# One TensorE body for all products: K and V by turns through one 32 KB buffer each, and wq, w1 and wo through the same two products

## The chip, the cores and the metric

The kernel runs on one core of one Trainium2 chip. The metric is the device time of one execution in microseconds (us). All numbers of a profile come from one profiled execution.

## The reference, cut to what matters

One decoding step for two rows of x. It mixes an attention over the last 4096 cached positions with a dense-Mish-dense block, by a sigmoid gate.

```python
# B, D, Hq, Hkv, Sk, Dh, F = 2, 512, 32, 8, 32768, 128, 1792;  W = 4096;  all fp32
q = (x @ wq).reshape(B, 1, Hq, Dh)                       # wq (512, 4096)
k, v = k_cache[:, :, Sk-W:], v_cache[:, :, Sk-W:]        # 8 heads, each used by 4 query heads
p = softmax(einsum("bhqd,bhkd->bhqk", q, k) * Dh**-0.5)
a = einsum("bhqk,bhkd->bhqd", p, v).reshape(B, 1, Hq*Dh) @ wo     # wo (4096, 512)
h = x @ w1 + b1                                          # w1 (512, 1792)
b = (h * tanh(softplus(h))) @ w2                         # w2 (1792, 512)
g = sigmoid((x * gate_w).sum(-1, keepdims=True))
out = g * a + (1 - g) * b
```

All of it is read once: 67 MB of K and V, 8.4 MB each of wq and wo, 3.7 MB each of w1 and w2, 91 MB together.

## The kernel before

**Layout.** Everything is stored for the kernel in rows, one to each of the 128 SBUF partitions. Three buffers `a`, `b`, `c` take 64 KB a partition each. K and V of one key-value head (both batch rows) stand side by side in one row of 64 KB (`kv_in[kv]`): the first 8192 numbers are K, the others V. Heads go by turns into `a` and `b`. `c` holds one half of wq, then the other, and at last w1, the first part of wo and a part of w2 (`w12`); the rest of wo follows in `a`, the rest of w2 in the end of `c`.

**The queue of loads.** All loads are issued by SyncE (SP), in the order of the code, by `load`. A load waits for a stage of TensorE (`"v0"`: the product with V of head 0 is done), so that its buffer is free; whatever stands behind it waits as well. The loads of heads 2 to 7 are issued while the load of another head is still on its way.

**TensorE.** `product` makes one output tile of 128x512 out of 16 matmuls: four column groups of 32 (`j`), each the sum over four chunks (`k`). In `step`, head `kv` goes through: wait for q (`q_in`) and for the data; the scores `sc`, 16 matmuls; `turn`, four transposes of the exponentials `p`; the product with V into `o`, 16 matmuls. `weights` does the same product with a half of wq or with w1, with x in the place of q. `ahead` runs over weights, two times two heads, weights, two times two heads, weights. `behind` is written out: the merge of the partial softmaxes (`lp`, `ol`), wo as 32 matmuls (`project`), w2 as 7 more and 7 blocks that are added up at the end (`finish`). An outer loop of two turns (`go`) passes over both parts once before it runs them.

**The other engines.** For each head VectorE takes the maxima of the scores (`mx`), ScalarE the exponentials and their sums, ScalarE copies the transposed `pT`, and after each second head VectorE picks the wanted parts of `o` (`om`, `od`, two heads in one instruction). After the last head `mx` is transposed (`mt`), the factors of the partial sums go over ScalarE, VectorE and GpSimd (`ms`, `top`) and back through TensorE (`ft`). Then `kf`, `kl` and the sums `lp` follow. Semaphores such as `q_in`, `p_in` and `pT_in` carry these hand-overs; the stages' names are counted in `STAGES`.

**The end.** The last three loads are pieces of w2 of 1 MB, 0.5 MB and 0.25 MB. After the last one `finish` ends, VectorE copies `fin` into `res`, and SP stores it.

Of the kernel before, what the change touches and what calls it, by code (L numbers as in the profile page):

```python
# [11 lines left out]
B = 2  # L12
# [17 lines left out]
FG = 4  # L30
HALF = 4
CHUNK = 8192
SMALL = DC * B + DC + FC
SCALE = DH ** -0.5
CAP = 20.0
CUTS = (0, 7, 11, 13, 14)
WO = (1, 6, 8)
ROWS = (24, 104)
WIDE = 2 * Q - B
STEP = Q + REP  # L40
TAIL = (FC - (NJ - 1) * FG) * P
GAPS = DC * (FG * P - TAIL) // D
FILLED = CHUNK + WO[0] * REP * D + (CUTS[1] - GAPS) * D

STAGES = ["gate"]
for _half in range(HKV // HALF):
    STAGES += [f"x{_half}s", f"x{_half}t"]
    for _kv in range(_half * HALF, (_half + 1) * HALF):
        STAGES += [f"s{_kv}", f"t{_kv}", f"v{_kv}"]
STAGES += ["tops", "factors", "x2s", "x2t", "shares", "outputs", "acc", "fin"]  # L50
# [3 lines left out]
class Line:  # L54
# [5 lines left out]
    def __call__(self, after, which, *args, credit=None, **kw):  # L60
        for mark in after[:-1]:
            self.e.wait_ge(*mark)
        ins = getattr(self.e, which)(*args, **kw)  # L63
        if after:
            ins._wait_ge(*after[-1])
        if credit is not None:
            ins.then_inc(credit, 1)
            return None
        ins.then_inc(self.sem, 1)
        self.n += 1  # L70
        return self.sem, self.n


def decode(nc, stored, small, wq, kv_in, w12, wo, w2, out):
    def sbuf(name, *shape):
        return nc.alloc_sbuf_tensor(name, [shape[0], *shape[1:]], F32).ap()
# [6 lines left out]
    a, b, c = (sbuf(n, P, 2 * CHUNK) for n in "abc")  # L83
# [8 lines left out]
    pick = sbuf("pick", P, BN)  # L92
    xg = sbuf("xg", P, DC, B)
    xs = sbuf("xs", P, B)
    g = sbuf("g", P, B)
    omg = sbuf("omg", P, B)
    qT = sbuf("qT", P, HKV, B, REP)
    p = sbuf("p", P, 512)
    pT = sbuf("pT", P, NT, P)
    om = sbuf("om", P, 2 * BN, DH)  # L100
# [7 lines left out]
    kl = sbuf("kl", P, HKV, BH)  # L108
    r = sbuf("r", P, HKV, B, REP)
    h, e, nu, de, ho = (sbuf(n, P, FC, B) for n in ("h", "e", "nu", "de", "ho"))  # L110
    sizes = (DC * Q, 2 * BN * STEP, HQ * Q, CUTS[1] * Q, (FC - CUTS[1]) * WIDE, WIDE)
    padded = sbuf("padded", P, sum(sizes))
    x32, qz, oT, actT, act2, fold2 = (
        padded[:, sum(sizes[:k]) : sum(sizes[: k + 1])] for k in range(len(sizes)))
    x32 = x32.rearrange("p (c q) -> p c q", q=Q)
    qz = qz.rearrange("p (y q) -> p y q", y=2)
    oT = oT.rearrange("p (k q) -> p k q", q=Q)
# [3 lines left out]
    sc = [bank(f"sc{y}", P, 512) for y in range(2)]  # L121
    pair = bank("o", P, 2, BN * DH)
# [3 lines left out]
    fb = bank("fb", P, 512)  # L126
    fin = fb[:, :P]
    zp = qb[:, :B]
    mt = qb[:HKV, 8 : 8 + P]
    ft = qb[:, 136 : 136 + HKV]  # L130
    lp = qb[:, 144 : 144 + HKV * BH].rearrange("p (k b h) -> p k b h", b=B, h=REP)
    ol = fb[:, P : P + HKV * BH].rearrange("p (k b h) -> p k b h", b=B, h=REP)

    names = ("data_a", "data_b", "data_c", "data_sm", "data_wo1", "data_wo2",
             "data_r1", "data_r2", "data_r3", "q_in", "p_in", "pT_in", "o_free")
    (d_a, d_b, d_c, d_sm, d_wo1, d_wo2, d_r1, d_r2, d_r3,
# [20 lines left out]
    load(b, kv_in[3], d_b, "v1")  # L157
    load(a, kv_in[4], d_a, "v2")
    load(b, kv_in[5], d_b, "v3")
    load(a, kv_in[6], d_a, "v4")  # L160
    load(b, kv_in[7], d_b, "v5")
    load(c[:, :FILLED], w12, d_c, "x1s")

    def flat(src, cuts, size):
        for f0, f1 in zip(cuts, cuts[1:]):
            yield (f1 - f0) * size, src[f0 * size * P : f1 * size * P].rearrange("(p x) -> p x", p=P)

    x = 0
    for sem, (cols, src) in zip((d_wo1, d_wo2), flat(wo, [f - WO[0] for f in WO], REP * D)):
        load(a[:, x : x + cols], src, sem, "v6")  # L170
        x += cols
    x = FILLED
    for sem, (cols, src) in zip((d_r1, d_r2, d_r3), flat(w2, [f - CUTS[1] for f in CUTS[1:]], D)):
        load(c[:, x : x + cols], src, sem)
        x += cols
# [7 lines left out]
    x_in = pool([blank, small_in], "tensor_copy", x32[:, :, ::RS], xT)  # L183
# [7 lines left out]
    fold2_in = dve([blank], "tensor_copy", fold2[:, Q - B : Q], fold[:, ::RS])  # L191
    prod = dve([small_in], "tensor_tensor", xg, xT, gw[:, :, None].to_broadcast([P, DC, B]), op=ALU.mult)
    gate_in = dve([prod], "tensor_reduce", xs, xg.rearrange("p c b -> p b c"), axis=AX.X, op=ALU.add)
    act([pe("gate")], "activation", g, zp, AF.Exp, scale=-1.0)
    t = dve([(act.sem, act.n)], "tensor_scalar_add", g, g, 1.0)
    t = dve([t], "reciprocal", g, g)
    gates_in = dve([t], "tensor_scalar", omg, g, -1.0, 1.0, op0=ALU.mult, op1=ALU.add)
    dve.e.sem_inc(o_free, 1)

    def head_in(kv, after):  # L200
        window = qz[:, kv % 2, :].rearrange("p (b n x) -> p b n x", n=NH, x=Q + REP)[:, :, :, :REP]
        pool(after, "tensor_copy", window, qT[:, kv, :, None, :].to_broadcast([P, B, NH, REP]),
             credit=q_in)

    def queries(i):
        act([pe(f"x{i}s")], "activation", p, sc[0], AF.Copy, scale=SCALE, credit=p_in)
        qt = pt.rearrange("p h (k b x) -> p h k b x", k=HALF, b=B)[:, :, :, :, 0]
        done = dve([pe(f"x{i}t")], "tensor_copy", qT[:, i * HALF : (i + 1) * HALF],
                   qt.rearrange("p h k b -> p k b h"))
        for kv in (i * HALF, i * HALF + 1):  # L210
            head_in(kv, [done])

    def head(kv):
        top_in = dve([pe(f"s{kv}")], "tensor_reduce", mx[:, kv : kv + 1], sc[kv % 2], axis=AX.X,
                     op=ALU.max, negate=True)
        act([top_in], "activation", p, sc[kv % 2], AF.Exp, bias=mx[:, kv : kv + 1],
            accum_out=ls[:, kv : kv + 1], credit=p_in)
        act([pe(f"t{kv}")], "copy", pT, pt, credit=pT_in)
        if (kv + 2) % HALF > 1:
            head_in(kv + 2, [pe(f"s{kv}")])  # L220

    def parts(kv):
        ov = om.rearrange("p (k m) d -> p k m d", m=BN)
        t = dve([pe(f"v{kv}")], "tensor_tensor", ov, pair.rearrange("p k (m d) -> p k m d", m=BN),
                pick[:, None, :, None].to_broadcast([P, 2, BN, DH]), op=ALU.mult)
        dve.e.wait_ge(*t)
        dve.e.sem_inc(o_free, 1)
        dve([], "tensor_reduce", od[:, kv - 1 : kv + 1], ov.rearrange("p k m d -> p k d m"),
            axis=AX.X, op=ALU.add)

    for kv in range(HKV):
        if kv % HALF == 0:
            queries(kv // HALF)
        head(kv)
        if kv % 2 and kv < HKV - 1:
            parts(kv)

# [8 lines left out]
    parts(HKV - 1)  # L246
# [3 lines left out]
    kl_in = dve([kf_in], "tensor_tensor", kl, kf, ls[:, :, None].to_broadcast(wide), op=ALU.mult)  # L250

    act([pe("x2s")], "copy", p[:, :TAIL], sc[0][:, :TAIL])
    act([], "copy", p[: Q * (NJ - 1), TAIL:], sc[0][: Q * (NJ - 1), TAIL:], credit=p_in)
    t = dve([pe("shares")], "reciprocal", r, lp)
    r_in = pool([t], "tensor_tensor", r, r, g[:, None, :, None].to_broadcast([P, HKV, B, REP]), op=ALU.mult)
    ht = pt.rearrange("p k (j b x) -> p k j b x", j=NJ, b=B)[:, :, :, :, 0]
    for j0, j1, nk in ((0, NJ - 1, FG), (NJ - 1, NJ, FC - (NJ - 1) * FG)):
        f0, f1 = j0 * FG, (j1 - 1) * FG + nk
        h_in = dve([pe("x2t")], "tensor_tensor", h[:, f0:f1, :].rearrange("p (j k) b -> p j k b", k=nk),
# [3 lines left out]
    o_in = dve([r_in, pe("outputs")], "tensor_tensor",  # L263
               oT.rearrange("p (k h) (b x) -> p k b h x", h=REP, x=RS)[:, :, :, :, 0], ol, r, op=ALU.mult)
    e_in = pool([h_in], "tensor_scalar_min", e, h, CAP)
    e_in = act([e_in], "activation", e, e, AF.Exp)
    ho_in = pool([gates_in], "tensor_tensor", ho, h, omg[:, None, :].to_broadcast([P, FC, B]), op=ALU.mult)
# [5 lines left out]
    pool([t], "tensor_tensor", actT[:, :, ::RS], nu[:, : CUTS[1]], ho[:, : CUTS[1]], op=ALU.mult)  # L273
    a_in = pool([], "tensor_tensor", act2[:, :, Q - B : Q], nu[:, CUTS[1] :], ho[:, CUTS[1] :], op=ALU.mult)
    asum_in = act([pe("acc")], "copy", p, acc)
    res_in = dve([pe("fin")], "tensor_copy", res, fin)
    store = nc.sync.dma_start(out, res[ROWS[0] : ROWS[1]]).then_inc(stored, 16)
# [14 lines left out]
    def product(out, lhs, block, mark=True):  # L292
        for k in range(NT):
            for j in range(NJ):
                mm(out[Q * j : Q * j + Q], lhs(k, j), block(k * NJ + j),
                   k == 0, k == NT - 1, mark=mark and k == NT - 1 and j == NJ - 1)
# [7 lines left out]
    def cut(t, k):  # L304
        return t[:, k * 512 : (k + 1) * 512]
# [138 lines left out]
```

## Time and profile before

| what | value |
|---|---|
| time, median of 3 runs | 220.59 us (219.42 to 221.84) |
| profiled execution, its own time | 220.39 us |
| its span, first to last instruction | 217.3 us |
| TensorE clock granted, mean | 0.819 |
| DMA: moved, mean rate | 91.31 MB, 420 GB/s |
| busy: TensorE matmul / VectorE / ScalarE / GpSimd | 53% / 10% / 7% / 3% |

The span leaves 3.1 us of the time outside (220.39 - 217.3). Of the views used below, the page's DMA queue row gives packets, MB, and the packets' time as a share of the 16 DMA engines' time; a row of the timeline gives start, length, engine, line of the kernel, operation, tiles and shapes, and in brackets the idle time of the engine ahead of it with what ended it. `PEq` is TensorE's own instruction queue.

### The profile page before, as it was taken

The page shows a single profiled execution, that of the slowest core. Times are in us where ns is not written, and L with a number is a line of the kernel's source. Part 1 is how long each engine was busy: PE and PEld are TensorE (multiplying, and loading weights), DVE is VectorE, ACT ScalarE, POOL GpSimd, SP SyncE. Part 2 cuts the span into 40 slices and gives each one's busy share as a digit, 9 for nine tenths or more (in the row PEclk, how much of TensorE's full clock was granted, in tenths as well). Part 3 has the DMA queues.
Part 4 walks back from the last instruction along what each step waited for, and adds up shares of the span by engine and source line. Part 5 has one row for each costly group of instructions (what it writes and reads, how often), then busy time and mean ns, then how long its engine had stood idle before and what let it go on. Part 6 is the DMA issues. An engine that isn't in the chain of part 4 may idle for free. (4 is left out here: it accounts for less than half of the span.)

```text
span 217.3 us, 1875 instructions
## 1 busy us (share of the span) xinstructions
PE 115.0 (53%) x816; PEld 36.6 (17%) x816; DVE 22.5 (10%) x37; ACT 15.6 (7%) x34; POOL 7.2 (3%) x28
## 2 busy tenths in 40 slices
PE   0029108552954009533779752287065918748895
PEld 0011002110220002101122220012021202215232
DVE  1010000100004000100106010010501001071100
ACT  2000100200020000200010020002002000211001
POOL 4000000000000000000000000000000000011200
PEclk9999755995579655996669998579958797999699
DMA  7998989896999898989899999999999999898993
GB/s 287 392 488 386 555 386 410 386 555 302 483 398 555 386 410 386 555 386 410 386 519 422 398 398 446 495 398 398 434 507 398 398 476 434 358 479 377 422 417 134
DMA packets 2546, 91.31 MB, mean 420 GB/s; under 512 B 416, under 2 KB 496, under 8 KB 752
## 3 DMA queue, kind: packets, MB, share of 16 engines
q1 hardware_dynamic: 2544, 91.28, 97.7%
q8 instruction: 2, 0.03, 0.1%
HBM read 91.24 MB, written 0.04 MB: 420 GB/s over the span
## 5 line engine op out<-in xcount | busy, mean ns | idle before, releaser
L286 PE MATMUL sc<-a,padded 128*32 128x512 f32 x128 | 21.6, 835 | 32.2 <-PEq L283 32.2
L286 PE MATMUL sc<-b,padded 128*32 128x512 f32 x128 | 23.6, 905 | 26.8 <-PEq L283 26.8
L286 PE MATMUL o<-b,pT 128*32 128x512 f32 x128 | 17.4, 692 | 3.1 <-PEq L283 3.1
L63 DVE TENSOR_REDUCE mx<-sc 128x1 f32<-128x512 f32 x8 | 5.5, 692 | 122.8 <-PE sc L286 122.8
L286 PE MATMUL o<-a,pT 128*32 128x512 f32 x128 | 15.9, 642 | 3.1 <-PEq L283 3.1
L301 PE MATMUL pt<-ident,p 128*128 128x128 f32 x44 | 6.9, 280 | 16.2 <-PEq L283 16.2
L63 ACT ACTIVATE p<-sc,mx 128x512 f32<-128x512 f32 x8 | 5.5, 687 | 137.6 <-DVE mx L63 137.6
L286 PE MATMUL sc<-c,padded 128*32 128x512 f32 x96 | 13.8, 727 | 0.9 <-PEq L283 0.9
L286 PEld LDWEIGHTS sc<-a,padded 128*32 128x32 f32 x128 | 5.6, 147 | 46.7 <-issue 46.7
L286 PEld LDWEIGHTS sc<-b,padded 128*32 128x32 f32 x128 | 5.9, 157 | 44.1 <-issue 44.1
L301 PEld LDWEIGHTS pt<-ident,p 128*128 128x128 f32 x44 | 4.6, 141 | 26.6 <-issue 26.6
L286 PE MATMUL qb<-xs,ones 128*128 128x2 f32 x2 | 0.6, 362 | 14.7 <-DVE xs L63 14.7
L63 DVE TENSOR_REDUCE od<-om 128x256 f32<-128x1024 f32 x4 | 7.9, 1977 | 0.6 <-DVE om L63 0.6
L286 PEld LDWEIGHTS o<-b,pT 128*32 128x32 f32 x128 | 4.9, 126 | 12.9 <-issue 12.9
L63 DVE TENSOR_TENSOR om<-o,pick 128x1024 f32<-128x1024 f32 x4 | 4.9, 1220 | 21.0 <-PE o L286 21.0
L286 PE MATMUL acc<-a,padded 128*32 128x512 f32 x56 | 6.8, 594 | 0.0
L286 PEld LDWEIGHTS o<-a,pT 128*32 128x32 f32 x128 | 4.7, 118 | 11.6 <-issue 11.6
L63 POOL COPY padded<-qT 128x16 f32<-128x16 f32 x8 | 1.5, 198 | 129.9 <-DVE qT L63 70.0
L63 ACT COPY pT<-pt 128x512 f32<-128x512 f32 x8 | 4.7, 586 | 6.5 <-PE pt L301 6.5
L286 PEld LDWEIGHTS sc<-c,padded 128*32 128x32 f32 x96 | 3.6, 128 | 8.9 <-issue 8.9
L286 PE MATMUL acc<-c,padded 128*32 128x512 f32 x22 | 4.3, 851 | 0.8 <-POOL padded L63 0.5
L286 PEld LDWEIGHTS qb<-xs,ones 128*128 128x128 f32 x2 | 0.5, 310 | 14.7 <-DVE xs L63 14.7
(60 smaller groups left out, 29.1 us busy)
## 6 DMA issues: line engine op xcount, KB each, us to landing
c<-in_wq SPq DMA_DIRECT2D x2, 4096.0 KB, 27.0
c<-in_w SPq DMA_DIRECT2D x1, 6400.0 KB, 40.8
a<-in_wo SPq DMA_DIRECT2D x1, 5120.0 KB, 32.0
a<-in_wo SPq DMA_DIRECT2D x1, 2048.0 KB, 36.5
c<-in_w SPq DMA_DIRECT2D x1, 1024.0 KB, 38.5
c<-in_w SPq DMA_DIRECT2D x1, 512.0 KB, 39.3
c<-in_w SPq DMA_DIRECT2D x1, 256.0 KB, 39.4
a<-in_kv SPq DMA_DIRECT2D x4, 29.6
```

The source lines that it names most:

```text
L63: ins = getattr(self.e, which)(*args, **kw)
L286: ins = T.matmul(out, lhsT, rhs, start=start, stop=stop)
L301: ins = T.transpose(pt[:, k, :], p[:, k * P : (k + 1) * P], ident)
```

## The change

K and V of a head become two loads of 4 MB, in rows of 32 KB: every K goes into `k0`, every V into `v0`. K of the next head is loaded once the scores of this head are done (`s`), V once the product with V is done (`v`). The two halves of wq go through the same two products (the second one in the place of V), so do w1 and the second half of wo, and at last the first half of wo. TensorE's program is one loop of 11 turns with branches for what differs, and a short end; the loop of two turns that passed over the code is gone. x, q and the attention's output are spread into windows of one shape (`lq`, `pT`) by GpSimd. The parts of `o` are picked after every head instead of every second one. The merge makes the weighted sum over `od` by two matmuls of 64x512 (`acc`, `fb`), from which VectorE picks (`oc`) and sums (`os`) before a transpose (`ot`). The gate's sum comes out of the matmul `lp`. A part of w2 comes early (`early`), before w1.

The core of the diff:

```diff
-    a, b, c = (sbuf(n, P, 2 * CHUNK) for n in "abc")
+    k0, v0 = (sbuf(n, P, CHUNK) for n in ("k0", "v0"))
+    rest = sbuf("rest", P, FC * D)
...
-    load(c[:, :CHUNK], wq[0], d_c)
+    load(k0[:, :HEAD], wqh, d_first)
+    load(k0[:, HEAD:], wqt, d_k)
     load(sm, small, d_sm)
-    load(a, kv_in[0], d_a)
-    load(b, kv_in[1], d_b)
-    load(c[:, :CHUNK], wq[1], d_c, "x0s")
-    load(a, kv_in[2], d_a, "v0")
...
+    load(v0, wq1, d_v)
+    for kv in range(HKV):
+        load(k0, kv_in[kv, 0], d_k, f"s{kv - 1}" if kv else "xs")
+        load(v0, kv_in[kv, 1], d_v, f"v{kv - 1}" if kv else "xv")
+    load(*flat(CUTS[0], CUTS[1]), d_early)
+    load(k0, w1, d_w1, f"s{HKV - 1}")
+    load(v0, wo1, d_v, f"v{HKV - 1}")
+    nc.sync.wait_ge(d_w1, 16)
+    nc.sync.sem_inc(d_k, 16)
...
+        t = dve([pe(f"v{kv}")], "tensor_tensor", om, o.rearrange("p (m d) -> p m d", m=BN),
+                pick[:, :, None].to_broadcast([P, BN, DH]), op=ALU.mult)
         dve.e.wait_ge(*t)
         dve.e.sem_inc(o_free, 1)
...
+        od_in = dve([], "tensor_reduce", od[:, kv, :], om.rearrange("p m d -> p d m"), axis=AX.X, op=ALU.add)
...
+    gaps_in = act([(d_w1, 16)], "copy", rest[:, : GAPS * D].rearrange("p (k x) -> p k x", k=DC),
+                  k0.rearrange("p (k x) -> p k x", k=DC)[:, :, (NJ - 1) * FG_P + TAIL :])
...
+    nc.sync.wait_ge(*gaps_in)
+    x = SPLIT * NJ * D
+    load(k0[:, :x], wo0[: P * x].rearrange("(p x) -> p x", p=P), d_k, "ws")
+    load(k0[:, x:], wo0[P * x :].rearrange("(p x) -> p x", p=P), d_split)
+    for k, sem in enumerate((d_r1, d_r2, d_r3), 1):
+        load(*flat(CUTS[k], CUTS[k + 1]), sem)
...
+    with T.Fori(0, 11, 1) as u:
         take(q_in, 1)
...
+        take(d_k, 16)
+        product(sc, lq, k0, SPLIT)
+        with T.If(u < 10):
+            turns()
             take(o_free, 1)
...
+            take(pT_in, 1)
+            take(d_v, 16)
+            product(o, pT, v0)
+            with T.If(u == 0):
+                turns()
+            with T.If(u == 8):
+                merge()
+            with T.If(u == 9):
+                T.wait_ge(*gaps_in)
+                project(0, CUTS[1], {0: a_in, GAPS: (d_early, 16)})
...
+    project(CUTS[1], ACC, {CUTS[1]: (d_r1, 16)})
...
-    with T.Fori(0, 2, 1) as go:
-        with T.If(go == 1):
-            ahead()
-        with T.If(go == 1):
-            behind()
```

SP's queue behind the last two heads, before: the loads of heads 6 and 7 into `a` and `b`, then `w12`, wo in two pieces, w2 in three, and the store.

```order
9 L147 DMA a<-in_kv 128x16384
10 L147 DMA b<-in_kv 128x16384
11 L147 DMA c<-in_w 128x12800
12 L147 DMA a<-in_wo 128x10240
13 L147 DMA a<-in_wo 128x4096
14 L147 DMA c<-in_w 128x2048
15 L147 DMA c<-in_w 128x1024
16 L147 DMA c<-in_w 128x512
17 L277 DMA out<-res 80x128
```

The same place now, from K and V of the last head (rows 18 and 19) on: seven blocks of w2, w1, the second half of wo, the first half of wo in two pieces, w2's last five blocks, the store.

```order
18 L150 DMA k<-in_kv 128x8192
19 L150 DMA v<-in_kv 128x8192
20 L150 DMA rest<-in_w 128x3584
21 L150 DMA k<-in_w 128x8192
22 L150 DMA v<-in_wo 128x8192
23 L150 DMA k<-in_wo 128x6144
24 L150 DMA k<-in_wo 128x2048
25 L150 DMA rest<-in_w 128x1024 x2
26 L150 DMA rest<-in_w 128x512
27 L303 DMA out<-res 80x128
```

Row 23 now waits for the product with w1 (`ws`), because it writes the buffer that w1 stands in; before, `w12` and wo went into buffers that the last heads and wq had left.

VectorE behind the last head, before: the maxima's merge stands ahead of the picking of heads 6 and 7, and `r` is made straight from the sums.

```order
20 L63 TENSOR_REDUCE mx<-sc 128x1 x2
21 L63 TENSOR_TENSOR mj<-ms 8x64
22 L63 TENSOR_REDUCE top<-mj 8x16
23 L63 TENSOR_TENSOR om<-o,pick 128x1024
24 L63 TENSOR_REDUCE od<-om 128x256
25 L63 TENSOR_TENSOR kf<-key,qb 128x64
26 L63 TENSOR_TENSOR kl<-kf,ls 128x64
27 L63 RECIPROCAL r<-qb 128x64
```

VectorE at the same place now: the last head's picking stands first, and `oc` and `os` have come in.

```order
30 L63 TENSOR_TENSOR om<-o,pick 128x512
31 L63 TENSOR_REDUCE od<-om 128x128
32 L63 TENSOR_TENSOR mj<-ms 8x64
33 L63 TENSOR_REDUCE top<-mj 8x16
34 L63 TENSOR_TENSOR kf<-key,qb 128x64
35 L63 TENSOR_TENSOR kl<-kf,ls 128x64
36 L63 RECIPROCAL r<-qb 128x64
37 L63 TENSOR_TENSOR oc<-acc,own 64x512
38 L63 TENSOR_TENSOR oc<-fb,own 64x512
39 L63 TENSOR_REDUCE os<-oc 64x128
```

On TensorE the transpose that reads `os` stands ahead of the product with w1, so that product now comes behind this whole row of VectorE; before, it came right behind the transpose `ft`.

More of the change, by code (lines that the diff above doesn't have):

```diff
@@ L35 @@
 CAP = 20.0
-CUTS = (0, 7, 11, 13, 14)
-WO = (1, 6, 8)
+HALF = 4
+FG = 4
+FG_P = FG * P
+TAIL = (FC - (NJ - 1) * FG) * P
+GAPS = DC * (FG_P - TAIL) // D
+CUTS = (GAPS, 9, 11, 13, 14)
+ACC = 11
+SPLIT = 3
 ROWS = (24, 104)
 WIDE = 2 * Q - B
[L40 to L50, printed above, removed]
+SHIFT = P + REP
+STAGES = ["xs", "xt", "xv", "xt2"]
+for _kv in range(HKV):
+    STAGES += [f"s{_kv}", f"t{_kv}", f"v{_kv}"]
+STAGES += ["tops", "factors", "shares", "outputs", "turned", "ws", "wt", "ov", "early", "h0", "acc", "fin"]
 AT = {name: k + 1 for k, name in enumerate(STAGES)}
@@ L58, in __init__, with __call__ @@
         self.n = 0
-    def __call__(self, after, which, *args, credit=None, **kw):
+    def __call__(self, after, which, *args, credit=None, by=1, **kw):
         for mark in after[:-1]:
@@ L198, in decode @@
-    dve.e.sem_inc(o_free, 1)
-    def head_in(kv, after):
[L201 to L206, printed above, removed]
-        qt = pt.rearrange("p h (k b x) -> p h k b x", k=HALF, b=B)[:, :, :, :, 0]
[L208 to L211, printed above, removed]
@@ L215, in head @@
+    first = queries(0, sc, "xs", "xt", [])
+    second = queries(1, o, "xv", "xt2", [first])
+    empty = pool([pe("xs")], "memset", lq, 0.0)
+    head_in(0, [empty, second])
+    for kv in range(HKV):
+        top_in = dve([pe(f"s{kv}")], "tensor_reduce", mx[:, kv : kv + 1], sc, axis=AX.X,
                      op=ALU.max, negate=True)
-        act([top_in], "activation", p, sc[kv % 2], AF.Exp, bias=mx[:, kv : kv + 1],
+        act([top_in], "activation", p, sc, AF.Exp, bias=mx[:, kv : kv + 1],
@@ L217, in head @@
             accum_out=ls[:, kv : kv + 1], credit=p_in)
[L218 to L225, printed above, removed]
+        if kv < HKV - 1:
+            head_in(kv + 1, [pe(f"s{kv}")])
+        else:
+            empty = pool([pe(f"s{kv}")], "memset", lq, 0.0)
+            x_windows(lq, q_in, 2, [empty])
@@ L290, in mm, with turn, product @@
             ins.then_inc(pe_sem, 1)
-    def product(out, lhs, block, mark=True):
+    def turn(out, src, eye, after=None, mark=True):
+        ins = T.transpose(out, src, eye)
+        if after is not None:
+            ins._wait_ge(*after)
+        if mark:
+            ins.then_inc(pe_sem, 1)
+    def product(out, lhs, t, split=None):
         for k in range(NT):
+            if k == split:
+                take(q_in, 1)
             for j in range(NJ):
-                mm(out[Q * j : Q * j + Q], lhs(k, j), block(k * NJ + j),
-                   k == 0, k == NT - 1, mark=mark and k == NT - 1 and j == NJ - 1)
@@ L298, in turn, with turns @@
-    def turn():
+                x = k * NJ + j
+                mm(out[Q * j : Q * j + Q], lhs[:, x * Q : x * Q + Q], t[:, x * 512 : (x + 1) * 512],
+                   k == 0, k == NT - 1, mark=k == NT - 1 and j == NJ - 1)
+    def turns():
         take(p_in, 1)
         for k in range(NT):
-            ins = T.transpose(pt[:, k, :], p[:, k * P : (k + 1) * P], ident)
-        ins.then_inc(pe_sem, 1)
-    def cut(t, k):
-        return t[:, k * 512 : (k + 1) * 512]
-    def weights():
-        take(d_c, 16)
-        product(sc[0], lambda k, j: x32[:, k, :], lambda k: cut(c, k))
-        turn()
@@ L312, in step, with merge @@
-    def step(y, t, sem):
+            turn(pt[:, k, :], p[:, k * P : (k + 1) * P], ident, mark=k == NT - 1)
+    def merge():
+        turn(mt, mx, ident)
+        turn(ft, ms.rearrange("k j r -> k (j r)"), ident[:HKV, :HKV], after=ms_in)
+        mm(lp, ones, kl, True, True, after=kl_in, mark=True)
+        kw = kf.rearrange("p k x -> p (k x)")
+        for y, dst in enumerate((acc, fb)):
+            mm(dst[: HKV * BH], kw, od[:, y * half : (y + 1) * half, :].rearrange("p k d -> p (k d)"),
+               True, True, mark=y == 1)
+        turn(ot.rearrange("p k b h -> p (k b h)"), os_, ident[: HKV * BH, : HKV * BH], after=os_in)
@@ L313, in step, with block, project @@
+    def block(f):
+        return rest[:, f * D : (f + 1) * D]
+    def project(f0, f1, after):
+        for f in range(f0, f1):
+            mm(acc[Q * (f % NJ) : Q * (f % NJ) + Q], actT[:, f, :], block(f), f < NJ, f >= ACC - NJ,
+               after=after.get(f), mark=f == f1 - 1)
+    T.wait_ge(d_first, 16)
+    T.wait_ge(*one)
+    with T.Fori(0, 11, 1) as u:
         take(q_in, 1)
-        take(sem, 16)
-        product(sc[y], lambda k, j: qz[:, y, k * Q : k * Q + Q], lambda k: cut(t, k))
@@ new lines, in finish, with output @@
+    def finish(lhsT, rhs, first=False, last=False, after=None):
+        for j in range(NJ):
+            y = j % 2 * (Q - B)
+            mm(fin[Q * j : Q * j + Q, :], lhsT[:, y : y + Q], rhs[:, j * P : (j + 1) * P],
+               first, last, after if j == 0 else None, last and j == NJ - 1)
+    def output(k, sem):
+        for f in range(CUTS[k], CUTS[k + 1]):
+            finish(act2[:, f - ACC, :], block(f), first=f == ACC, last=f == FC - 1,
+                   after=(sem, 16) if f == CUTS[k] else None)
@@ L390 @@
+    output(2, d_r2)
+    finish(fold2, p, after=asum_in)
+    output(3, d_r3)
 def kernel(**inputs):
```

238 lines of the change are left out of this document (97 added, 141 removed).

## Prediction

> **What bounds the kernel now.** First the page: the span, the busy shares, the DMA queues, and the chain that ended last.
>
> ```profile
> span 217.3 us, 1875 instructions
> PE 115.0 (53%) x816; PEld 36.6 (17%) x816; DVE 22.5 (10%) x37; ACT 15.6 (7%) x34; POOL 7.2 (3%) x28
> q1 hardware_dynamic: 2544, 91.28, 97.7%
> q8 instruction: 2, 0.03, 0.1%
> DMA 18%; PE 3%; SPq 0%; DVE 0%; issue 0%
> ```
>
> No engine is busy for more than 53%, and the DMA engines are for 97.7%: the kernel is a stream of 91 MB. Both versions read the same bytes. The 2.3% that are left are 5 us, most of them at the two ends, so more than that can't be won; what can be lost is anything that leaves the queue empty. The last long piece of the chain is a load, which agrees.
>
> Then the cost of a load. I ask the DMA view for two stretches in which only one sort of packet starts: from 53 to 59.5 us the second half of wq (rows of 32 KB), from 63 to 76 us a head (rows of 64 KB).
>
> ```profile
> q1 hardware_dynamic: 87, 2.85, 101.5%
> q1 hardware_dynamic: 91, 5.96, 106.0%
> ```
>
> A packet of 32 KB takes 1.015 x 16 x 6.5 / 87 = 1.213 us of one DMA engine, one of 64 KB 1.060 x 16 x 13 / 91 = 2.423 us. A load of 128 rows gives each of 16 engines eight rows, so 4 MB take 9.7 us.
>
> **Smaller rows.** 64 rows of 64 KB per DMA engine (eight heads) become 128 of 32 KB: 64 x (2 x 1.213 - 2.423) = 0.2 us. There are 29 DMAs in place of 18, and some rows of 8 to 24 KB in place of 40 and 50 KB. I take +0.4 us for both, between 0 and 0.8.
>
> **One buffer each: does the queue run empty while heads stream?** K of the next head is issued when this head's scores are done. By then V of this head is on its way, 9.7 us of it. So it comes in time if the product plus the dead time from an issue to flowing data is under 9.7 us. The timeline of TensorE has the product: eight that follow an idle time of 5 us or more, and two that follow shorter ones.
>
> ```profile
> 15.24 6.59 PE L286 MATMUL sc<-c,padded 128*32 128x512 f32 x32
> 33.63 5.93 PE L286 MATMUL sc<-a,padded 128*32 128x512 f32 x32 [10.35 <-PEq L283]
> 41.27 0.63 PE L301 MATMUL pt<-ident,p 128*128 128x128 f32 x4 [1.71 <-PEq L283]
> 42.66 3.64 PE L286 MATMUL o<-a,pT 128*32 128x512 f32 x32 [0.77 <-PEq L283]
> 52.93 6.52 PE L286 MATMUL sc<-b,padded 128*32 128x512 f32 x32 [6.63 <-PEq L283]
> 62.56 5.12 PE L286 MATMUL o<-b,pT 128*32 128x512 f32 x32 [0.77 <-PEq L283]
> 81.89 5.69 PE L286 MATMUL sc<-a,padded 128*32 128x512 f32 x32 [14.21 <-PEq L283]
> 101.22 6.27 PE L286 MATMUL sc<-b,padded 128*32 128x512 f32 x32 [6.88 <-PEq L283]
> 139.88 5.71 PE L286 MATMUL sc<-b,padded 128*32 128x512 f32 x32 [8.26 <-PEq L283]
> 159.19 6.29 PE L286 MATMUL sc<-a,padded 128*32 128x512 f32 x32 [6.85 <-PEq L283]
> 178.61 5.12 PE L286 MATMUL sc<-b,padded 128*32 128x512 f32 x32 [5.00 <-PEq L283]
> ```
>
> After a long idle time the product takes 5.12 to 6.59 us, 6.0 in the mean of the eight; soon after other work 3.64 to 5.12. For the dead time, SP's first load, its store, and the landing times of `c`:
>
> ```profile
> 0.72 0.39 SPq L147 DMA_DIRECT2D c<-in_wq  x1
> out<-res SPq DMA_DIRECT2D x1, 40.0 KB, 1.5
> DMA to landing us min/median/max: 13.4/39.3/40.8
> q8 instruction: 2, 0.03, 0.4%
> ```
>
> The store of 40 KB on an empty queue lands after 1.5 us. The first load, also on an empty queue, lands after 13.4 us, of which 9.7 are its packets. The last row is the first 30 us again: two instruction packets, 0.004 x 16 x 30 = 1.9 us of DMA time, so about 0.95 us on an engine; with that off, 2.75 us stay. The dead time is between 1.5 and 2.75 us; I take 1.8, nearer to the store. Then a half of a head needs 6.0 + 0.1 + 1.8 = 7.9 of 9.7 us, and in the worst case 6.6 + 0.1 + 2.75 = 9.45. The queue stays filled, K and V alike (the exponentials and `pT` come 3 us after the scores, before V lands). The cover left is 1.8 us, 0.25 at worst; what it costs without it is the second rival. The two halves of wq at the start go through the same test.
>
> The Trainium skill speaks against smaller loads: "DMA: Bandwidth & Descriptors", section "Anatomy of one DMA", puts about 2.0 us of fixed cost on each DMA, mostly the confirmation of the last write. By that figure the cover would be 1.6 in place of 1.8 us; as a cost of every queued load it would be 11 x 2.0 = 22 us more, and the packet rows above, which leave no room between loads, speak against that reading.
>
> **The one place where the queue does run empty.** The first half of wo can be issued only after `ws`. From the moment T at which V of the last head lands, the queue still holds seven blocks of w2 (1.75 MB), w1 and the second half of wo (4 MB each): 4.2 + 9.7 + 9.7 = 23.6 us. Against it stands a chain. The rows for it are those of the old merge and two groups:
>
> ```profile
> 190.72 0.26 ACT L63 COPY ms<-qb 8x128 f32<-8x128 f32 x1 [4.03 <-PE qb L333]
> 191.01 0.21 DVE L63 TENSOR_TENSOR mj<-ms 8x64 f32<-8x64 f32 x1 [6.52 <-ACT ms L63]
> 191.26 0.24 DVE L63 TENSOR_REDUCE top<-mj 8x16 f32<-8x64 f32 x1
> 191.59 0.59 POOL L63 TENSOR_TENSOR ms<-ms,top 8x64 f32<-8x64 f32 x2 [45.71 <-DVE top L63]
> 192.21 0.31 ACT L63 ACTIVATE ms<-ms 8x128 f32<-8x128 f32 x1 [1.23 <-POOL ms L63]
> 192.57 0.22 PE L334 MATMUL qb<-ident,ms 8*128 8x8 f32 x1 [1.88 <-ACT ms L63]
> 194.95 0.22 DVE L63 TENSOR_TENSOR kl<-kf,ls 128x64 f32<-128x64 f32 x1
> 198.92 0.43 PE L286 MATMUL qb<-kl,ones 128*128 128x64 f32 x2
> 201.45 1.31 PE L286 MATMUL acc<-c,padded 128*32 128x512 f32 x8 [0.36 <-DVE padded L63]
> L63 DVE TENSOR_TENSOR om<-o,pick 128x1024 f32<-128x1024 f32 x4 | 4.9, 1220 | 21.0 <-PE o L286 21.0
> L63 DVE TENSOR_REDUCE od<-om 128x256 f32<-128x1024 f32 x4 | 7.9, 1977 | 0.6 <-DVE om L63 0.6
> ```
>
> - V's product, 0.1 + 6.0 us. Ahead of it TensorE idles some 3.7 us with the transposes in between, which no row shows exactly; the ends are 3.64 and 6.6.
> - `om` and `od` of one head, half the size: 0.6 + 1.0, with gaps 1.7 us. They now stand ahead of `mj`.
> - From `mj` to the end of `ft`: 191.01 to 192.79, 1.8 us; then `kf` and `kl` 0.5, `lp` 0.5: 2.8 us.
> - The two new matmuls of 64x512. No row has one. A product is eight groups of four matmul passes side by side, so (32 records for 16 matmuls) a pass of 512 columns takes 3.64 / 8 = 0.46 to 6.6 / 8 = 0.83 us, and two fp32 matmuls are four passes without a neighbour: 1.8 to 3.3 us. TensorE comes from 4 us with little work, so I take 3.3, with 0.2 for the hand-over 3.5.
> - `oc` twice 512 columns, as `om`: 1.25; `os` sums 1024, as `od`: 2.0; the transpose, the loop's jump and the next waits 0.7. Together 3.95 us.
> - The product with w1, after an idle time: 6.0 us.
>
> T to `ws`: 6.1 + 1.7 + 2.8 + 3.5 + 3.95 + 6.0 = 24.05 us. With 1.8 us of dead time, data flow 25.85 us after T, against 23.6 of cover: an empty queue for **2.2 us**. With all short ends (3.7, 2.0 for the matmuls, 5.1, dead time 1.5) it is 20.75 and no gap; with all long ones (6.7, 3.5, 6.6, 2.75) 28.0 and 4.4 us.
>
> Two of these terms hang on TensorE's clock after a pause. The rows: 3.64 us right after work, 5.12 to 6.59 after 5 us without. The Trainium skill, "TensorE: Matmul & The Clock Gate", section "Why this matters for your kernels", warns of idle gaps over about 3 us between bursts, after which the clock drops to half. By this rule V's product is slow, as I took it, and the gap stays 2.2; if 3.7 us with transposes in them don't count as idle, that product takes 3.64 and the gap is nothing.
>
> **What lies beside other work.** More, shorter `om` and `od` (eight pairs of 1.7 us for four of 3.2), GpSimd's windows, and the copy of w2's part by ScalarE stand beside TensorE's waits for data; without that cover the copy alone would be worth 1.2 us (1024 columns, ScalarE's 512 take 0.59). TensorE's end is the same: four short matmuls after the last 0.25 MB, `res`, the store.
>
> **Instruction packets.** A load is complete with its last engine, so a packet of 0.95 us that holds one engine delays all. TensorE's program shrinks from 175 matmuls to 73. If neither packet is left, 0.95 us is won; if one is, nothing. I take -0.3.
>
> **Sum**, on the profiled execution: 220.39 + 0.4 + 2.2 - 0.3 = **222.7 us**, with the 3.1 us outside the span unchanged. The profiled time stands 0.2 us below the median of the three runs, 220.59.
>
> **The rivals.** *No gap:* the chain to `ws` is short enough. 220.39 + 0.4 - 0.95..0 = 219.8 to 220.8. For it: 3.64 us is common in the trace; against it: nearly all of its short ends are needed together. *The queue runs empty in every half:* the second rival, on the slower side. It decides once product and dead time are over 9.7 us, that is a dead time over 3.0 us with the slowest products; the first load's full 3.7 us would do it. Then 18 halves lose 0 to 0.7 us each; at 0.4, with the gap 2 us longer, 222.7 + 7.2 + 1.9 = 231.8. Against it: the rows above give 2.75 at most. The skill's fixed cost, paid by every load, would fall under this rival. *The loop's jumps miss:* the change doesn't do what it says, and code is loaded again in the loop. At 0.95 us a time this hides in the cover of 1.8 us, except ahead of `ws`: 223.7 or more. Against it: before loops too, and shows two packets in all, both in the first 30 us. *Faster:* 97.7% leaves only the ends; both packets gone, no gap, a run at the low edge: 218.
>
> **How the numbers follow.** The forecast, a gap of 1 to 3.5 us: 0.55, with 221.3 to 224.3. No gap 0.26; empty in every half 0.09; missing jumps 0.04; faster 0.06. A measurement of this kernel tells about 1% from no change, 2.2 us: under 218.4 or over 222.8. The forecast's range lies about half over that: 0.27 same, 0.28 slower. With no gap (0.26, same) and the two slower rivals this makes 0.06 faster, 0.53 same, 0.41 slower. The range, 219.5 to 225.5, takes in the case without a gap and the long ends of the chain; the empty queue in every half is left out, and so are the faster case and the worst of the jumps.
>
> **What would show it.** One stretch with idle DMA engines, some 200 to 205 us into the span, ended by the issue of wo's first half right after `ws`; from 15 to 175 us a DMA share as before. `os` ends 11 to 12 us after the last V product. If the DMA share drops in each half, the second rival is right; if the chain from T to `ws` is under 22 us, the first. The forecast is wrong in kind if the queue's packet time changes, or if TensorE waits for its own program.

## The result, and the profile after

The changed kernel takes **228.87 us** (median of 4 runs, 228.23 to 229.89) against 220.2 us (median of 4, 219.42 to 221.84): a ratio of 1.0388, with a 95% interval of 1.0311 to 1.0465. It is slower, and outside the range of the prediction. The profiled execution took 228.28 us with a span of 226.4, at a granted clock of 0.827 (before 0.819). The ratios in this document leave out an execution in a slower state, more than 1.5% above the fastest of its kernel (e1_go and e6_own have one each, their highest time), which the medians and ranges still count.

The page of the kernel after: span, busy shares, the DMA and GB/s rows of the 40 slices (5.66 us each), and the queues.

```profile
span 226.4 us, 1928 instructions
PE 124.9 (55%) x779; PEld 37.0 (16%) x779; DVE 28.7 (13%) x54; ACT 16.6 (7%) x35; POOL 9.4 (4%) x34
DMA  6999999799999999999999999999999999997893
GB/s 250 434 429 452 399 431 457 289 446 365 440 330 440 376 457 417 411 457 376 434 417 446 399 440 434 423 434 394 417 440 440 405 420 454 452 446 259 360 404 155
q1 hardware_dynamic: 4128, 91.28, 96.0%
q8 instruction: 1, 0.02, 0.0%
```

The same 91.28 MB, now spread over a span that is 9.1 us longer. The DMA row shows a slice with a 7 from 40 to 45 us and a 7 and an 8 from 204 to 215; the GB/s row shows more than the tenths do: below 380 in slices 8, 10, 12, 14 and 19, all while heads stream. Stretches of 20 us make that readable, first of the kernel before, then of the one after (columns: window, length, busy time of PE, PEld, DVE, ACT and POOL, clock, DMA share, and last GB/s).

```profile
40.00:60.00 20.00, 10.79 (x68) 3.13 (x68) 0.80 (x2) 1.36 (x3) 0.20 (x1) 0.74 0.98 423
60.00:80.00 20.00, 5.75 (x36) 1.74 (x36) 3.37 (x3) 1.36 (x3) 0.00 (x0) 0.73 1.01 439
80.00:100.00 20.00, 9.96 (x68) 2.94 (x68) 0.69 (x1) 1.36 (x3) 0.00 (x0) 0.84 1.04 449
100.00:120.00 20.00, 15.50 (x102) 4.63 (x103) 3.95 (x3) 1.96 (x4) 0.00 (x0) 0.75 0.97 419
120.00:140.00 20.00, 8.49 (x76) 3.04 (x79) 0.88 (x2) 1.36 (x3) 0.53 (x3) 0.85 0.98 426
140.00:160.00 20.00, 10.67 (x72) 3.02 (x75) 3.85 (x3) 1.36 (x3) 0.20 (x1) 0.84 1.02 442
160.00:180.00 20.00, 12.52 (x76) 3.58 (x72) 0.69 (x1) 1.36 (x3) 0.00 (x0) 0.76 0.97 421
```

```profile
40.00:60.00 20.00, 11.56 (x72) 3.40 (x68) 2.43 (x3) 1.36 (x3) 0.24 (x1) 0.76 0.94 387
60.00:80.00 20.00, 11.38 (x72) 3.32 (x68) 2.43 (x3) 1.36 (x3) 0.24 (x1) 0.76 0.98 395
80.00:100.00 20.00, 10.18 (x76) 3.12 (x72) 2.42 (x3) 1.36 (x3) 0.24 (x1) 0.84 0.98 419
100.00:120.00 20.00, 10.49 (x76) 3.08 (x71) 2.43 (x3) 1.36 (x3) 0.24 (x1) 0.84 1.00 424
120.00:140.00 20.00, 12.58 (x80) 3.45 (x76) 2.43 (x3) 1.36 (x3) 0.24 (x1) 0.78 1.00 423
140.00:160.00 20.00, 11.75 (x80) 3.65 (x72) 2.42 (x3) 1.36 (x3) 0.24 (x1) 0.83 1.01 424
160.00:180.00 20.00, 11.12 (x68) 3.39 (x64) 2.42 (x3) 1.36 (x3) 0.24 (x1) 0.74 0.98 423
206.00:210.00 4.00, 3.15 (x24) 0.93 (x20) 0.25 (x2) 0.64 (x2) 0.45 (x2) 0.84 0.66 197
```

Between 40 and 180 us the mean was 431 GB/s before and is 414 now. Over 140 us that is 2.5 MB too little, or 5.7 us at the old rate. In single rows of before the rate swings too, since 64-KB packets are counted where they fall; its mean over the stretch is what compares. The DMA share hides most of this (it is 0.98 at 395 GB/s, and 1.01 at 439 before), since packets on engines that have just been refilled last longer: from 63 to 66 us 27 of 32 KB start at a share of 97.9%, so that one takes 0.979 x 16 x 3 / 27 = 1.7 us, where the prediction found 1.2 in a full stream. The last row is the one gap that was forecast: 206 to 210 us.

Where the 9.1 us of span are, from the same two traces: V of the last head is used from 185.34 us on, where the last head's scores began at 178.61 before; the same bytes have landed at both points, so 6.7 us are lost until then. 2.2 us are lost ahead of the first half of wo, and 0.2 at the end. Outside the span 1.9 us are left, where the profiled execution of before had 3.1. 6.7 + 2.2 + 0.2 - 1.2 = 7.9 us, and 220.39 + 7.9 is the measured 228.28. But the 1.2 us are no gain of the change: in 28 of 30 later executions of the kernel before 1.8 to 2.2 us lie outside the span, and 3.0 and 3.4 in the other two.

How a hole of the stream arises, in SP's rows (start, duration, the issue) beside TensorE's:

```profile
28.48 0.33 SPq L150 DMA_DIRECT2D v<-in_kv  x1
41.82 0.33 SPq L150 DMA_DIRECT2D k<-in_kv  x1
36.31 5.45 PE L312 MATMUL sc<-k,padded 128*32 128x512 f32 x32 [6.39 <-PEq L309]
```

K of head 0 is complete at 36.2 us on its last engine, the scores start at 36.31 and take 5.45 us, and K of head 1 is issued right after, at 41.82. By then V of head 0, issued at 28.48 and queued behind K, is about to end on 15 of 16 engines (landings from 41.9 to 42.4 us). This is the worst of the holes: K of head 1 lands 1.8 us late. Of the 16 loads of the heads eight are issued less than 2.8 us ahead of the drain, and lose 0.2 to 1.8 us each; of the other eight one loses 0.8 (at a lead of 2.9) and seven nothing (0.05 or less). The leads and losses here and below are read from the packets and landings of the 16 engines in the traces.

### The profile page after: what moved, and what is told of

Same layout as the page of the kernel before. It is cut to its first block, busy times and chain, and to the rows that moved or that the text cites. A ratio compares the mean times of both kernels' runs of the same rounds, so it can differ in the third digit from the quotient of the medians.

```text
span 226.4 us, 1928 instructions
## 1 busy us (share of the span) xinstructions
PE 124.9 (55%) x779; PEld 37.0 (16%) x779; DVE 28.7 (13%) x54; ACT 16.6 (7%) x35; POOL 9.4 (4%) x34
## 3 DMA queue, kind: packets, MB, share of 16 engines
q1 hardware_dynamic: 4128, 91.28, 96.0%
## 5 line engine op out<-in xcount | busy, mean ns | idle before, releaser
L312 PE MATMUL sc<-k,padded 128*32 128x512 f32 x352 | 62.4, 874 | 60.2 <-PEq L309 60.2
L312 PE MATMUL o<-v,padded 128*32 128x512 f32 x320 | 46.0, 727 | 15.9 <-PEq L309 15.9
L312 PEld LDWEIGHTS sc<-k,padded 128*32 128x32 f32 x352 | 16.1, 153 | 103.8 <-issue 103.8
L312 PEld LDWEIGHTS o<-v,padded 128*32 128x32 f32 x320 | 13.3, 129 | 41.9 <-issue 41.9
L63 DVE TENSOR_TENSOR om<-o,pick 128x512 f32<-128x512 f32 x8 | 5.5, 692 | 64.9 <-PE o L312 64.9
L63 DVE TENSOR_REDUCE od<-om 128x128 f32<-128x512 f32 x8 | 8.3, 1043 | 1.2
L63 POOL COPY padded<-qT 128x64 f32<-128x64 f32 x8 | 1.9, 236 | 137.9 <-PE sc L312 128.6
L63 ACT COPY padded<-pt 128x512 f32<-128x512 f32 x8 | 4.7, 585 | 6.5 <-PE pt L319 6.5
L63 POOL MEMSET padded<- 128x528 f32 (+2 forms) x4 | 3.1, 766 | 34.0 <-PE sc L312 26.9
L312 PE MATMUL acc<-rest,padded 128*32 128x512 f32 x22 | 3.8, 595 | 0.0
L63 DVE TENSOR_TENSOR om<-om,sc 128x512 f32<-128x512 f32 x1 | 0.7, 687 | 10.3 <-PE sc L312 10.3
## 6 DMA issues: line engine op xcount, KB each, us to landing
k<-in_wo SPq DMA_DIRECT2D x1, 3072.0 KB, 10.3
```

What stands on the lines that cost most here:

```text
L312: ins = T.matmul(out, lhsT, rhs, start=start, stop=stop)
```

## The experiments

Three theories stood against each other. **A:** a straggler; the one instruction packet of 16 KB at 33 us holds one DMA engine, and all later holes follow from that (a straggler is the engine that ends a load last). **B:** a load has to be issued about 3 us before the queue drains, not 1.8, and most halves don't have that. **C:** 32-KB packets in alternating buffers are slower by themselves. "Lead" is how long before the middle one of the 16 engines ends the packets of the load ahead the next load is issued; "loss" is by how much its landing there then comes later than 9.69 us after the landing ahead.

### e1_go: the code loaded before the stream

```diff
+    with T.Fori(0, 2, 1) as go:
+        with T.If(go == 1):
             <the first two waits and the loop of 11 turns>
+        with T.If(go == 1):
             <the short end>
```

> The new kernel with the old kernel's outer loop of two turns around TensorE's program, which passes over the code once before it runs it, so that the packet of code that held one DMA engine at 33 us comes while the first half of wq is loaded. Theory A (the straggler: that packet made one engine finish the first K 3.4 us after the others, and the queue's cover was lost from there on): the long idle stretch at 42 us goes and most of the later ones, 222.5 to 225. Theory B (a load needs some 3 us from its issue to flowing data while others are on their way, more than the 1.8 us that were taken, so halves with a slow product lose time with or without a straggler): the stretch at 42 us shrinks, others stay, 226 to 228. Theory C (packets of 32 KB that alternate between K and V are slower by themselves): no change, 228 to 229.

Measured: 230.26 us (227.72 to 233.12), ratio 1.0506 (1.0422 to 1.0589). The packet moved to 4.5 us, and the stretch from 40 to 60 us is whole again. The holes come back elsewhere:

```profile
40.00:60.00 20.00, 13.27 (x68) 3.54 (x68) 2.06 (x3) 1.24 (x3) 0.23 (x1) 0.66 1.01 433
60.00:80.00 20.00, 11.22 (x68) 3.21 (x68) 2.10 (x3) 1.36 (x3) 0.01 (x1) 0.74 0.98 403
160.00:180.00 20.00, 13.35 (x68) 3.58 (x68) 2.42 (x3) 0.90 (x4) 0.61 (x2) 0.66 0.98 396
```

433 GB/s where 387 stood, but 403 and 396 later. In the profiled execution (227.72 us, within B's 226 to 228) V of the last head lands 1.7 us earlier than in the change, about what the hole at 42 us had cost, and the gap ahead of wo takes most of that back: from there to the last load it is 40.5 us (39.1 in the change). The median lies above what any of the three theories expected. The straggler makes one hole and not the loss: A falls as the main cause.

### e2_half: products of half the length

```diff
-        for k in range(NT):
+        for k in (0, NT - 1):
```

> The new kernel with half of every product left out: chunks 0 and 3 of the four, 8 of 16 matmuls, so its values are not the reference's; all loads and hand-overs stay. The next load is issued some 2.5 us earlier in each half, and the chain ahead of wo is 5 us shorter. Theories A and B: cover of over 5 us in each half, no idle stretch while heads stream and none ahead of wo: 219 to 221.5. Theory C: the heads lose as much as before, only the gap ahead of wo goes: 225.5 to 227.

Measured: 219.38 us (219.15 to 220.69, 10 runs), ratio 0.9983 (0.9954 to 1.0013), the span 217.3 as before the change. All 16 leads are 5.0 to 5.7 us and all losses 0.00 within 0.03. The page:

```profile
span 217.3 us, 1256 instructions
DMA  7998989999999999999999999999999999989993
```

Between the first slice and the last none is under 8; the gap ahead of wo is gone too. The same packets in the same buffers now run without a hole, so C falls: with leads of 5 us and more nothing is lost. This is also the floor of the stream, 219.4 us.

### e3_early: the gap at wo filled with w2's pieces

```diff
     load(v0, wo1, d_v, f"v{HKV - 1}")
+    load(*flat(CUTS[1], CUTS[2]), d_r1)
+    load(*flat(CUTS[2], CUTS[3]), d_r2)
...
-    for k, sem in enumerate((d_r1, d_r2, d_r3), 1):
-        load(*flat(CUTS[k], CUTS[k + 1]), sem)
+    load(*flat(CUTS[3], CUTS[4]), d_r3)
```

> The new kernel with two of w2's last three pieces (0.5 MB each, 2.5 us of loading) issued ahead of wo's first half, where they need not wait for the product with w1. All theories agree that the queue runs empty there for 2 to 2.6 us: 226.3 to 227.3, as the stretch is filled and the end is not longer. If that stretch is not what the end waits for: 228 to 229.

Measured: 229.1 us (226.56 to 229.9), ratio 1.0421 (1.0362 to 1.048), not to be told from the change itself. In its profile the gap is gone and the last byte lands at 219.7 us, 4.1 earlier than in the changed kernel. But what lands last is now wo, and behind it stands a product:

```profile
216.81 3.64 PE L313 MATMUL sc<-k,padded 128*32 128x512 f32 x32 [1.83 <-PEq L310]
221.35 0.69 DVE L63 TENSOR_TENSOR p<-om,acc 128x512 f32<-128x512 f32 x1 [0.15 <-PE acc L313]
223.12 0.36 SPq L304 DMA_DIRECT2D out<-res  x1
```

The store goes out 3.4 us after the last byte (223.12 - 219.7), where it was 1.04 (224.82 - 223.78). So 2.4 us are given back at the end, and the median shows no gain. The expected 226.3 to 227.3 us was met by the profiled execution, but by luck, and missed by the median: in that execution the heads lost less, and V of the last head is used from 182.51 us on in place of 185.34. Of the 4.1 us 2.8 are from there, and only the rest can be the gap; the 2.4 us at the end take all of it.

### e4_split: two issues a half, the first one early

```diff
-        load(k0, kv_in[kv, 0], d_k, f"s{kv - 1}" if kv else "xs")
+        stage = f"s{kv - 1}" if kv else "xs"
+        halves(k0, kv_in[kv, 0], d_k, stage + "h", stage)
...
-                   k == 0, k == NT - 1, mark=k == NT - 1 and j == NJ - 1)
+                   k == 0, k == NT - 1, mark=k in (1, NT - 1) and j == NJ - 1)
...
-        take(d_k, 16)
+        take(d_k, 32)
```

Each of K, V, wq's and wo's second half goes in two loads of 2 MB; the first is issued once the product is through with its columns, at half of its time. The 3-MB piece of wo's first half is cut in two as well, so there are 19 more DMAs.

> The new kernel with K, V, the second half of wq and of wo each loaded in two halves of 2 MB; the first half is issued when the first two of the four chunks of the product before it are done, some 2.5 to 3 us earlier; 18 more DMAs. Theory B: the first half is in the queue in time, the idle stretches while heads stream go, 222 to 224.5, and the gap ahead of wo stays. Theory A: the straggler's 3.4 us are only partly covered, 224 to 226.5. Theory C: nothing is won, 228.5 to 230.

Measured: 223.49 us (222.23 to 223.93), ratio 1.0161 (1.0111 to 1.0211). The stream's rows:

```profile
40.00:60.00 20.00, 10.72 (x66) 2.90 (x64) 2.43 (x3) 1.23 (x3) 0.24 (x1) 0.83 1.00 430
60.00:80.00 20.00, 11.98 (x68) 3.46 (x68) 2.43 (x3) 1.25 (x4) 0.24 (x1) 0.74 1.01 431
120.00:140.00 20.00, 11.83 (x68) 3.49 (x68) 2.42 (x3) 1.36 (x3) 0.24 (x1) 0.74 1.01 431
160.00:180.00 20.00, 11.18 (x72) 3.23 (x76) 2.42 (x3) 1.36 (x3) 0.77 (x2) 0.84 1.02 435
200.00:204.00 4.00, 3.15 (x28) 1.07 (x24) 0.25 (x2) 0.64 (x2) 0.24 (x1) 0.95 0.59 187
```

428 to 435 GB/s in every 20 us from 40 to 180, a 2-MB load about every 4.86 us, with the full products and with the instruction packet still at 33 us. The gap ahead of wo stays (last row). The split wins 5.4 us of the median, within B's range (222 to 224.5) and about what the heads had lost; V of the last head lands 5.8 us earlier than in the change. B holds, and A is covered once there is lead.

### e5_lead: the lead set by hand

Half products again, and a memset on GpSimd of growing length between the scores of a head and the issue of the next K.

```diff
+        pool([], "memset", scratch[:, : (1000, 1600, 2150, 2700, 3250, 3800, 4350)[kv]], 0.0, credit=late)
...
+            nc.sync.wait_ge(late, kv)
```

> The kernel with half products (8 of 16 matmuls in each, values not the reference's), in which every K is issued some 5.2 us before the V ahead of it has landed. Now GpSimd fills an unused buffer after each score product, for some 0.9 us after the first head to 3.8 us after the seventh, and SP issues the next K only then, so the lead falls from head to head from about 4.2 to about 1.2 us. Theory B (a load needs some 3 us from issue to flowing data under load): no loss down to a lead of 3 us, then a loss that grows by about the time that is missing, 1.5 to 2 us at the last. As predicted before (dead time 1.8 us): no loss down to 1.8 us, at most 0.6 us at the last.

Measured: 226.9 us (one run), span 224.9. Seven stretches of 10 us, each from about the end of the load ahead, in which the delayed K runs (for heads 1 to 7):

```profile
41.40:51.40 10.00, 3.64 (x16) 0.68 (x16) 1.73 (x2) 0.00 (x0) 0.00 (x0) 0.67 1.08 465
60.80:70.80 10.00, 3.64 (x16) 0.69 (x16) 1.74 (x2) 0.00 (x0) 0.00 (x0) 0.50 1.06 455
80.20:90.20 10.00, 3.42 (x16) 0.68 (x16) 1.73 (x2) 0.00 (x0) 0.00 (x0) 0.67 1.03 442
99.60:109.60 10.00, 3.64 (x16) 0.68 (x16) 1.74 (x2) 0.00 (x0) 0.00 (x0) 0.67 1.03 436
119.10:129.10 10.00, 3.64 (x16) 0.68 (x16) 1.74 (x2) 0.00 (x0) 0.00 (x0) 0.67 0.98 383
140.00:150.00 10.00, 3.64 (x16) 0.68 (x16) 1.73 (x2) 0.00 (x0) 0.17 (x1) 0.50 0.93 377
161.40:171.40 10.00, 3.64 (x16) 0.68 (x16) 1.73 (x2) 0.00 (x0) 0.00 (x0) 0.67 0.96 393
```

To each row belong these values, read from the packets and landings on the 16 engines:

| head | lead us | loss us | issue to last landing, less 9.7 us |
|---|---|---|---|
| 1 | 3.95 | 0.0 | |
| 2 | 3.51 | 0.0 | |
| 3 | 3.00 | 0.04 | |
| 4 | 2.35 | 0.20 | 4.3 |
| 5 | 1.06 | 1.39 | 5.0 |
| 6 | -0.23 | 2.06 | 2.7 |
| 7 | 1.22 | 0.87 | 4.9 |

The rate falls from 465 to 377 GB/s as the lead falls, and the loss begins at 3 us. Lead plus loss is the time from issue to flowing data on the middle engine: 1.8 us for head 6, whose load came when most engines had run empty, 2.1 to 2.6 for heads 4, 5 and 7. The last column takes the last engine, which a product waits for (for heads 1 to 3 the load waits its turn in the queue, and the column says nothing): 2.7 us for head 6, 4.3 to 5.0 for the others, their wait for their turn included. B holds in that the loss begins at 3 us and passes what a dead time of 1.8 us allows (1.39 us were lost at a lead of 1.06, where it gives 0.7). It is not right that the loss grows by all of the time that is missing: at a lead of 1.22, 1.8 us short of 3, it is 0.87. The dead time is no constant.

### e6_own: a buffer of its own for wo's first half

```diff
-    k0, v0 = (sbuf(n, P, CHUNK) for n in ("k0", "v0"))
+    k0, v0, w0 = (sbuf(n, P, CHUNK) for n in ("k0", "v0", "w0"))
...
-    load(k0[:, :x], wo0[: P * x].rearrange("(p x) -> p x", p=P), d_k, "ws")
...
+    load(w0[:, :x], wo0[: P * x].rearrange("(p x) -> p x", p=P), d_own)
```

The load no longer waits for the product with w1 and stands right behind wo's second half; the heads are as in the change.

> The new kernel with a buffer of its own for the first half of wo, so that it and all of w2's rest are issued right behind the second half of wo, without waiting for the product with w1; its product stands behind the loop, which has 10 turns. If the gap ahead of wo is worth what the trace shows: 2 to 2.6 us less than the new kernel, 226 to 227. If the end waits for TensorE instead: less than 1 us, 228.

Measured: 226.32 us (224.84 to 229.21), ratio 1.026 (1.0206 to 1.0315). Against the 228.87 of the change that is 2.5 us, the size of the gap. This is a rough figure: without the highest execution the median is 225.61, 3.3 us less than the change, and either ratio has an interval of 0.5 to 0.8% to each side. In the profiled execution (229.21 us, the highest) the heads lose 3 us more than in the change, but no slice is under 8 from the second to the last but one, so the gap is gone:

```profile
DMA  7999989899999999999999999999999999999993
```

The traces show the size of the gap without the heads' losses, as the time from the landing of V of the last head to that of the last load, both on the middle engine: 39.1 us in the change and 39.3 in e4_split, 36.6 here, 36.5 in e2_half and e7_both, and 36.4 before. So the gap is worth 2.5 us there.

### e7_both: e4_split and e6_own together

> Both repairs: K, V, wq's and wo's second half in two loads each, the first one issued after two of four chunks, and a buffer of its own for the first half of wo. Theory B: no idle stretch is left, the stream is that of the kernel before with 0.4 to 1 us more for packets: 219.5 to 221.5, no difference from before that three to five rounds can tell. If the repairs overlap, or something else was lost: 222 to 224.

Measured: 220.47 us (220.27 to 221.53, 12 runs) against 220.02 (219.21 to 221.39, 17 runs), ratio 1.0029 (1.0008 to 1.005). The same three places of its profile:

```profile
40.00:60.00 20.00, 10.97 (x64) 2.98 (x64) 2.43 (x3) 0.66 (x2) 0.24 (x1) 0.74 1.01 432
160.00:180.00 20.00, 11.73 (x73) 3.78 (x77) 2.43 (x3) 1.36 (x3) 0.78 (x2) 0.83 1.01 434
200.00:204.00 4.00, 3.15 (x25) 0.85 (x18) 0.00 (x0) 0.64 (x2) 0.24 (x1) 0.85 1.00 424
```

Neither the holes nor the gap are left. 228.87 - 5.4 (e4_split) - 2.5 (e6_own) would be 221.0, and 220.47 was measured: the two losses are separate, and together they are all of the slowdown but 0.5 us. The pair does not beat the kernel before. With half products the same stream took 219.38 us, so little was to be had.

## Why the prediction was wrong

**The step that failed: "the queue stays filled, K and V alike".** It set product + dead time against 9.7 us with a dead time of 1.8 us, "between 1.5 and 2.75 us; I take 1.8, nearer to the store", and took the heads as 0. They cost 5.7 to 6.7 us. The form of the test was right, and two of its inputs were not.

- *The dead time.* A store of 40 KB says when its own bytes are there. What a product waits for is the last of 16 engines of a load of 4 MB, and e5_lead puts that at 2.7 to 5.0 us. The first load had shown 3.7 us, 2.75 without the 0.95 of an instruction packet. For a queue that is empty on all engines this upper end was right: in e2_half, where no such packet comes then, the first 4 MB take 2.4 us more than their packets. It is not for a queue that is just draining. A load loses nothing from a lead of 3.0 us on, and the product leaves 9.7 - 6.0 - 0.1 = 3.6 us, so the cover was 0.6 us and not 1.8.
- *The spread.* The test took each load as landing at one time. After a hole the engines end as much as 2.8 us apart in e5_lead (0.4 ahead of its first hole), the next product starts with the last of them, and the next lead is shorter by that, which is more than the cover. So the leads were -0.1 to 4.8 us.

**The rival that came true** is the second one, the empty queue in every half, which had a chance of 0.09. Its threshold, a dead time over 3.0 us, was passed on the last engine. Its price, 18 halves at 0.4 us or 7.2 us, stands beside 5.7 to 6.7 measured, since many halves lost little. Its 1.9 us of longer gap did not come.

**The size of the gap ahead of wo** was right: 2.2 us forecast, 2.2 us by the trace to the last engine and 2.5 us by e6_own. It stood at 206 to 210 us, not at 200 to 205, since the stream ran 6.7 us late. Its parts, on TensorE and VectorE (start, duration, what is done, idle time before):

```profile
185.34 3.64 PE L312 MATMUL o<-v,padded 128*32 128x512 f32 x32 [1.74 <-PEq L309]
193.52 1.92 PE L312 MATMUL acc<-od,kf 128*64 128x512 f32 x2
195.24 1.91 PE L312 MATMUL fb<-od,kf 128*64 128x512 f32 x2
198.50 1.89 DVE L63 TENSOR_REDUCE os<-oc 64x128 f32<-64x1024 f32 x1
201.41 6.52 PE L312 MATMUL sc<-k,padded 128*32 128x512 f32 x32 [0.60 <-PEq L309]
207.99 0.80 SPq L150 DMA_DIRECT2D k<-in_wo  x2
```

`os` ends at 200.39, 11.4 us after V's product (188.98); 11 to 12 were forecast. The two matmuls take 3.6 us with their overlap (3.5 taken). V's product took 3.64 us, not 6.0, and w1's 6.52, not 6.0. From the landing of V (185.2) to `ws` (207.97) it is 22.8 us against 24.05. By that alone the gap would have been smaller, but the load of 3 MB lands 10.3 us after its issue, of which 7.3 are its packets: its start cost 3.0 us and not 1.8. So two errors of this term cancel, and that the figure came out is luck. The rule on idle gaps that the prediction named, the Trainium skill's "TensorE: Matmul & The Clock Gate", section "Why this matters for your kernels", had two readings there. The last V's product ran fast, with 1.74 us of idle time right before it, as by the second, and the missing gap that was tied to it did not follow. But the traces decide for neither: of the nine products from `v0` up to there in the same trace, after 1.0 to 2.8 us of idle time, three took 3.64 us and six 5.0 to 5.3, and the last V's took 6.10 us in e1_go and 5.34 in e4_split.

**Packets.** +0.4 us was forecast and nothing came: e2_half has the span of before to the tenth. The 2.0 us of fixed cost that the prediction took from the Trainium skill, "DMA: Bandwidth & Descriptors", section "Anatomy of one DMA", stand there for DMAs that GpSimd issues; the loads here are issued by SyncE. No run shows such a cost for each queued load: up to V of the last head e7_both has 17 more loads than e2_half, and this V lands 0.9 us later. **Instruction packets.** One is left in the loop's time, at 33 us, ahead of the hole of 1.8 us at 42 us, but e1_go shows that moving it wins nothing in the median while leads are short. **Jumps**: no further packet of 16 KB on the queue that brought the code (q8) follows to the end of the span. From 37 us on the view of the DMAs lists one instruction packet of 8 KB on another queue (q14), of 0.3 us at 204.9 us; what it brings is not shown. **Outside the span** 3.1 us were taken as fixed. This came from one unusual execution: 1.8 to 2.2 us are common for the kernel before too, so the base of the sum was some 1.2 us high.

The page of before could not have shown the hole that was coming, but it had the warning: its loads of heads were issued 3 us or more before the drain (head 5 the shortest, and it lost 0.1 us), so no row of it measured a load that has to start on a draining queue.

## What to carry to other kernels

Where a stream is to stay full, compare the time from the release of a buffer to the drain of the queue with the whole time that a load takes beyond its packets, to its *last* engine, and take that from a large load of the same kernel rather than from a small store. If buffers must shrink, release and refill them in parts: a second issue at half of the product kept the stream at 428 to 435 GB/s, and the 17 more loads cost about 0.9 us in all. A gap filled by moving other transfers ahead is only worth what the work behind the new last transfer leaves of it.

## What was not expected of the hardware

- A load lost nothing on its way when it was issued 3 us or more before the queue drained (0.04 us at most), and up to 2.1 us on the middle engine when it wasn't (e5_lead). Where the engines are apart the bound is less sharp: with full products loads with a lead of 3.0 to 3.5 us lost up to 0.4 us (e3_early, e6_own).
- A queue that drains while the next load is issued does not go on evenly: in e5_lead the 16 engines end up to 2.8 us apart after that, against 0.4 us before, and the spread is handed on to the loads behind. A stream without holes can have a spread as well (1.3 to 1.8 us in the kernel before).
- The straggler was made mostly by such a start. K of head 0 was issued at 20.51 us with a lead of 1.5 us. 15 engines take its first packet between 21.9 and 22.8 us; the sixteenth takes it at 24.07, 3.6 us after the issue, and for 1.8 us. It is two packets behind when the instruction packet of 16 KB comes at 33.1 us and holds it for 0.93 us; its last packet of K then takes 1.7 us in place of 1.2. So K of head 0 is complete at 36.2 us, 3.4 us after the 15 others (32.2 to 32.8), and the instruction packet's part in that is about 1.4 us. The part of the profile on DMA, from 30 to 37 us, has the packet:

```profile
q8 instruction: 1, 0.02, 0.8%
```

0.008 x 16 engines x 7 us is 0.9 us. Why one engine of 16 starts a load so late was not found.
